# A linear-attention and feed-forward kernel: its steps put into an order written out for each engine, with whole query loads, one mask multiply and tables built on GpSimd

## The chip, the cores and the metric

The kernel runs on one core of a Trainium2 chip. A core has five engines that run side by side and meet through semaphores: TensorE (PE, matrix products; PEld is its loading of weights), VectorE (DVE), ScalarE (ACT), GpSimd (POOL) and SyncE (SP, which here only issues transfers). Sixteen DMA engines move data between HBM and the core's memory SBUF. Matrix products are written to PSUM, which has eight banks. The metric is the time of one execution on the device in microseconds (us); lower is better.

## The reference

Inputs are q, k, v of shape (4, 8, 768, 64) (batch, heads, positions, head size), a decay `lam` for each head, and the feed-forward weights `w_in` (512 x 2048), `w_out` (2048 x 512) and `alpha` (2048). All are float32.

```python
# attention, for each batch and head, in blocks of 64 positions
intra = (qb @ kb.T * Dmask) @ vb              # Dmask[i,j] = lam**(i-j) for i >= j, else 0
inter = (qb * lam_pow) @ kv_state             # lam_pow[i] = lam**(i+1)
out   = intra + inter
kv_state = lam**64 * kv_state + (kb * rev_pow).T @ vb
# feed-forward over the 3072 positions, x = heads side by side (512 columns)
h = x @ w_in
s = sin(alpha * h)
g = h + s * s / (alpha + 1e-9)
return g @ w_out
```

## The kernel before

**Units and groups.** The attention works in blocks of 128 positions in place of 64, two blocks (256 positions) at a time. One *unit* is one batch, four heads and 256 positions: 24 units, `u` = 0 to 23. Four units fill one *group* `g` of 512 rows for the feed-forward part: groups 0 to 5. `where(u)` gives the mapping. Rows of a unit are held with even and odd positions apart (`two`, `par`).

**Steps of a unit** (names as in the order of steps, with the unit's number behind them):

- `ld..q`, `ld..k`, `ld..v`: loads of 256 KB each on SP's queue into one of three buffers per kind (`load`). Before, the queries of units 1 to 7 (the set `Q4`) came as two transfers of 64 partitions each, in runs of 1024 B; all others come as one transfer in runs of 512 B.
- `cq`, `ck`: casts to bf16 (`cast`). `sv`: v times a table of inverse decays R, to bf16 (`scale_v`, on POOL).
- `tq`, `tk`: transposes on PE, and `e0`, `e1`: their copies out of PSUM, for units 0 to 8. For units 9 to 23 there is one DMA transpose instead, `dt`, on SP's queue (`turn_dma`).
- `sc`: scores, 16 small products into a pair of PSUM banks `s`. `m0`, `m1`: the causal mask, one multiply on DVE for each half of the scores (`domask`); the results are bf16.
- `kv`: the products of keys and scaled values. `bx` or `d0`, `d1`, `n0`, `n1`, `kc`: decay and carrying of the state, with copies on ACT and arithmetic on POOL (DVE for `bx` of units 3 to 7).
- `in`, `io`: products of the carried state and of the masked scores into the pair of banks `okv`. `oe`: the result times a table ET, into `xt` of the group (`outev`, DVE).
- From unit 8 on, `step` u is one PE block: the `in` and `io` products of unit u-1 and the `sc` and `kv` products of unit u.

**Steps of a group.** `f1_g_f`: one of 16 first products (four matmuls of 128x512 into one of four banks `f`; group 0's `f` = 0 comes in two halves, of units 0 and 1, and of units 2 and 3). `sn`: the sine on ACT. `sq`: the square, on ACT or POOL. `g`: the sum into `gall` on DVE, which frees the bank. `f2_g_m_j`: a quarter of one of the four second products of a group (again four matmuls of 128x512). `ev`: its copy on ACT into one of three buffers `ob`. `out`: its store, two transfers on SP's queue. The last one, `f2_5_3`, comes in two halves of 256 columns (`end0`, `end1`, `send0`, `send1`; `make_f2_end`, `f2send`); `send1` has one transfer on SP and one on ACT.

**Weights.** `wi0` to `wi3` (columns of `w_in`: 256, 512, 512, 768) and `wo0` to `wo3` (four of 16 row blocks of `w_out` each) are loaded by transfers that POOL issues and that cast to bf16.

**Tables.** `lamb` spreads `lam` over the partitions by a product on PE, `tabc` copies it out, `tab1` raises it to powers (POOL), `tabm` and `tab2` make E and its inverse R (DVE). `tabd` multiplies an identity that PE has put into PSUM (`eye`) with E on DVE, giving ED, and `tab0` spreads this over partitions by a product; `tab3` and `tab4` copy it out as ET and LBD.

**Matmuls without a reader.** 35 matmuls on constants (`warm`, tile `bz`): nine of 512 columns ahead of everything, 26 of 256 columns that a planner places.

**What sets the order.** All steps are created as `Op`s with the engines they may run on, what they wait for and which buffers they take and give back. `Plan.run` walks through time by its own costs and picks, for each engine that is free, the ready step with the lowest due time `vt`; `TUNE` shifts due times step by step and fixes engines. The steps are then emitted in that order, and each engine executes its instructions strictly in the order emitted, waiting on semaphores where needed. SP's queue is such an order too: what stands behind a waiting issue waits with it. `GATES` holds unit 5's first load until `wo1` has landed, and unit 8's until `f1_0_8` has run.

The chip sees no trace of the planner but the resulting order. In it PE has, around the first feed-forward tile:

```
... in1 io1 tq4 sc3 kv3 tk4 in2 io2 warm x5 in3 io3 f1_0_0_0 kv4 sc4 f1_0_0_1 in4 f1_0_1 ...
```

and the ends of SP's and ACT's orders are

```
SP:  ... out_5_2 out_5_0 send0 out_5_1 send1
ACT: ... ev_5_2 ev_5_0 end0 ev_5_1
```

Of the kernel before, what the change touches and what calls it, by code (L numbers as in the profile page):

```python
# [16 lines left out]
class Op:  # L17


    def __init__(self, name, cost, after, vt, emit, take=(), give=(), lag=0.08, mode=None,  # L20
                 dma=None, gives=None, behind=None, drain=9):
        self.name, self.cost, self.vt, self.emit = name, cost, vt, emit
        self.after = [a for a in after if a is not None]
        self.take, self.give, self.lag, self.mode = take, give, lag, mode
        self.dma, self.gives, self.owed, self.behind = dma, gives or {}, {}, behind
        self.drain = drain
        self.start = self.done = self.eng = self.lent = None
        self.bank, self.ins = {}, None


class Plan:
# [3 lines left out]
    BEGIN, LAND, DEPTH = {"SP": 0.4, "POOL": 2.0}, 1.7, 6  # L35
    HEAD = 0.75
    FETCH = (14.5, 20.5, 27, 48, 56, 66.5, 76.5, 86, 98.5, 108.5, 121, 131.5, 142.5, 157)
# [10 lines left out]
    def run(self):  # L48
        kids, left, ready_t = {}, {}, {}
        for op in self.ops:  # L50
            left[op] = len(set(op.after))
            ready_t[op] = 0.0
            for a in set(op.after):
                kids.setdefault(a, []).append(op)
        seq = {op: i for i, op in enumerate(self.ops)}
        pool = {e: [] for e in self.ENG}
        future = [(0.0, seq[op], op) for op in self.ops if not left[op]]
        heapq.heapify(future)
        free = dict.fromkeys(self.ENG, self.HEAD)
        queue = {"SP": [], "POOL": []}  # L60
        returns, order = [], []
        t, last, mode, n = 0.0, 0.0, None, 0

        def finish(op, at):
            op.done = at
            for who, kind in op.give:
                who.owed[kind] = who.owed.get(kind, who.gives.get(kind, 1)) - 1
                if not who.owed[kind]:
                    for b in who.bank[kind]:
                        heapq.heappush(returns, (at, kind, b))  # L70
            for k in kids.get(op, ()):
                ready_t[k] = max(ready_t[k], at + op.lag)
                left[k] -= 1
                if not left[k]:
                    heapq.heappush(future, (ready_t[k], seq[k], k))

        landing, flying = [], [0]

        def active(at):
            act = [q for q in queue.values() if q and q[0][1] <= at + 1e-9]  # L80
            return act, sum(q[0][0].dma[1] for q in act)

        while n < len(self.ops):
            while last < t - 1e-9:
                act, whole = active(last)
# [11 lines left out]
                for q in act:  # L97
                    q[0][2] -= rate * step * q[0][0].dma[1] / whole
                    if q[0][2] <= 1e-6:
                        op, land = q.pop(0)[0], last + step + self.LAND  # L100
                        finish(op, land)
                        if op.eng == "SP":
                            heapq.heappush(landing, land)
                            flying[0] -= 1
# [6 lines left out]
            while future and future[0][0] <= t + 1e-9:  # L111
                op = heapq.heappop(future)[2]
                for e, _ in op.cost:
                    heapq.heappush(pool[e], (op.vt, seq[op], op))
            for e in self.ENG:
                if free[e] > t + 1e-9:
                    continue
                kept, got = [], None
                while pool[e]:
                    item = heapq.heappop(pool[e])  # L120
                    op = item[2]
                    if op.start is not None:
                        continue
                    if all(len(self.banks[k]) >= op.take.count(k) for k in op.take) and (
                            op.behind is None or op.behind.start is not None) and (
                            e != "SP" or (flying[0] <= op.drain and
                                          flying[0] + len(landing) < self.DEPTH)):
                        got = op
                        break
                    kept.append(item)  # L130
                    if e == "SP" and flying[0] > op.drain:
                        break
                for item in kept:
                    heapq.heappush(pool[e], item)
                if got is None:
                    continue
                op, c = got, dict(got.cost)[e]
                if e == "PE" and op.mode is not None:
                    c += 0.09 * (op.mode != mode)
# [7 lines left out]
                n += 1  # L147
                if op.dma:
                    queue[e].append([op, t + c + self.BEGIN[e], op.dma[0]])
                    flying[0] += e == "SP"  # L150
                else:
                    finish(op, t + c)
            nxt = [v for v in free.values() if v > t + 1e-9]
            nxt += [x[0][0] for x in (future, returns) if x]
            act, whole = active(t)
            nxt += [t + q[0][2] * whole / q[0][0].dma[1] for q in act]
            nxt += [f + x for f in self.FETCH for x in (0, self.HOLD)]
            nxt += landing[:1]
            nxt += [q[0][1] for q in queue.values() if q and q[0][1] > t + 1e-9]
            nxt = [v for v in nxt if v > t + 1e-9]  # L160
            if not nxt:
                raise RuntimeError("stuck: " + ", ".join(o.name for o in self.ops if o.start is None)[:500])
            t = min(nxt)
# [4 lines left out]
def kernel(  # L168
# [26 lines left out]
    SF = set()  # L195
    TUNE = {
        "lam": (990.8, 'ACT'), "iden": (0.3, 'POOL'), "eye": (0, 'PE'), "lamb": (7.8, 'PE'),
        "tabc": (388.5, 'DVE'), "tab1": (40.4, 'POOL'), "tabm": (448, 'DVE'), "tabd": (-18.6, 'DVE'),
        "tab2": (-57.7, 'DVE'), "tab0": (-7.6, 'PE'), "tab4": (19.8, 'DVE'), "tab3": (6.2, 'ACT'),
        "alq": (957.4, 'ACT'), "alpha": (-8.9, 'PE'), "alphav": (-46.8, 'DVE'), "ld0q": (-7.4, 'SP'),  # L200
# [1150 lines left out]
```

## Time and profile before

| what | value |
|---|---|
| median of 3 runs | 219.5 us |
| all runs | 221.01, 219.5, 218.84 us |
| span of the profiled execution, first to last instruction | 218.1 us |
| the profiled execution's own time | not listed apart from the three runs; the span is 1.4 us below their median |
| PE busy | 205.9 us (94%), 2042 matmuls in the records |
| ACT / DVE / POOL busy | 140.4 / 124.6 / 122.8 us |
| moved by DMA | 33.65 MB in 60460 packets, mean 154 GB/s |

The profile is one execution. "Busy" is the time in which an engine runs an instruction; an engine at 94% over the whole span can still wait in one stretch and be the limit in another, so the prediction cuts the span into stretches. The clock row gives the TensorE clock that was granted, in tenths (9 is 90% or more). Some matmul records are missing from the trace, so counts of matmuls are a little low. A line such as "L717 POOL CAST qk<-st_k" names the source line, the engine, the operation, and what is written from what.

### The profile page before, as it was taken

What the parts mean: (1) busy time and instruction counts of PE and PEld (TensorE: products, weight loads), DVE (VectorE), ACT (ScalarE), POOL (GpSimd) and SP (SyncE); (2) the same over time, 40 slices, a digit from 0 to 9 for tenths busy, and PEclk for the clock granted to TensorE, in tenths of its full rate; (3) what the DMA queues carried; (4) which work ended last, traced back from release to release, by engine and by line L of the source; (5) the groups of instructions that cost most, each with busy time, mean ns of one, the idle gap of its engine ahead of it and who ended that gap; (6) DMA issues with size and microseconds to landing.
All of it is one profiled execution on the core that took longest, in us unless ns stands there. A gap on an engine that the chain in (4) does not pass through costs nothing.

```text
span 218.1 us, 5252 instructions
## 1 busy us (share of the span) xinstructions
PE 205.9 (94%) x2042; PEld 105.1 (48%) x2070; DVE 124.6 (57%) x203; ACT 140.4 (64%) x253; POOL 122.8 (56%) x201
## 2 busy tenths in 40 slices
PE   8786999999999999999999999999999999999992
PEld 3354544455536554455645545445445444444461
DVE  3678686537659973477767864738625643543000
ACT  4374698575499754876948778558726877775111
POOL 4569699948999999988899591313111001030000
PEclk9999999999999999999999999999999999999999
DMA  5999999998999992899999992202222022111253
GB/s 168 254 256 217 207 200 215 259 255 233 291 174 181 298 314 64 174 263 195 290 219 223 298 186 49 48 3 50 48 51 48 2 51 48 28 37 35 48 120 72
DMA packets 60460, 33.65 MB, mean 154 GB/s; under 512 B 18051, under 2 KB 57491, under 8 KB 60435
## 3 DMA queue, kind: packets, MB, share of 16 engines
q1 hardware_dynamic: 56096, 29.04, 59.1%
q0 software_dynamic: 4224, 4.19, 11.7%
q8 instruction: 16, 0.26, 0.5%
q10 hardware_dynamic: 114, 0.07, 0.1%
q14 instruction: 10, 0.07, 0.1%
HBM read 27.27 MB, written 6.29 MB: 154 GB/s over the span
## 4 chain that ended last, share of the span: by engine, by line
PE 70%; DMA 13%; POOL 6%; ACT 4%; issue 3%; SPq 2%; DVE 1%; POOLq 0%; ACTq 0%; DVEq 0%
PE ops L962 30%; PE hps L926 28%; DMA st_v<-in_v_dram 7%; DMA st_k<-in_k_dram 6%; PE okv L962 3%; PE sp L773 2%; PE okv L896 2%; SPq L698 2%; ACT s L933 2%; POOL qk L717 2%; PE okv L883 1%; POOL vb L723 1%; DVE gall L945 1%; ACT s L940 1%; POOL s L942 1%
## 5 line engine op out<-in xcount | busy, mean ns | idle before, releaser
L945 DVE SCALAR_TENSOR_TENSOR gall<-s,r_sb,hps 128x512 bf16<-128x512 bf16 (+1 forms) x97 | 70.1, 740 | 55.0 <-ACT s L940 33.9
L926 PE MATMUL hps<-xt,w_in_sb 128*128 128x512 bf16 (+1 forms) x371 | 90.6, 377 | 1.9 <-DVE gall L945 0.5
L933 ACT ACTIVATE s<-hps,alpha_sb 128x512 bf16<-128x512 f32 (+1 forms) x97 | 64.6, 679 | 34.4 <-PE hps L926 31.1
L962 PE MATMUL ops<-w_out_sb,gall 128*128 128x512 bf16 (+1 forms) x358 | 81.6, 370 | 1.0 <-issue 0.6
L962 PEld LDWEIGHTS <-gall 128*128 128x128 bf16 x400 | 38.3, 98 | 41.4
L926 PEld LDWEIGHTS <-w_in_sb 128*128 128x128 bf16 x388 | 36.7, 98 | 44.3 <-issue 2.7
L942 POOL TENSOR_TENSOR s<-s 128x512 bf16<-128x512 bf16 x24 | 24.8, 1041 | 39.7 <-ACT s L933 39.6
L940 ACT ACTIVATE s<-s 128x512 bf16<-128x512 bf16 (+1 forms) x73 | 44.5, 623 | 1.4
L782 DVE TENSOR_TENSOR sm<-sp,mask 128x512 bf16<-128x512 f32 x48 | 32.6, 684 | 6.1 <-PE sp L773 6.1
L723 POOL TENSOR_TENSOR vb<-st_v,R 128x512 bf16<-128x512 f32 x24 | 25.0, 1045 | 8.6 <-DMA st_v<-in_v_dram 6.2
L968 ACT COPY ob<-ops 128x512 f32<-128x512 f32 x21 | 12.2, 582 | 19.1 <-PE ops L962 18.9
L832 POOL TENSOR_TENSOR kvx<-kva,kvs 128x128 f32<-128x128 f32 x32 | 14.6, 457 | 14.8 <-ACT kva L817 14.5
L835 POOL TENSOR_TENSOR kvbd<-kvx,LBD 128x256 bf16<-128x256 f32 x32 | 19.6, 614 | 2.5
L913 DVE TENSOR_TENSOR xt<-okv,ET 128x512 bf16<-128x512 f32 x24 | 16.5, 686 | 3.5 <-PE okv L896 3.5
L999 PE MATMUL bz<-const-bfloat16-1.0 128*128 128x256 bf16 (+1 forms) x35 | 9.6, 343 | 1.7 <-PEq L1335 0.8
L717 POOL CAST qk<-st_q 128x512 bf16<-128x512 f32 x16 | 9.6, 614 | 1.4 <-PE okv L807 1.4
L773 PE MATMUL sp<-qt 64*64 64x128 bf16 x384 | 10.0, 221 | 0.0
L717 POOL CAST qk<-st_k 128x512 bf16<-128x512 f32 x16 | 9.7, 615 | 0.0
L896 PE MATMUL okv<-sm,vb 64*64 64x128 bf16 x384 | 9.7, 218 | 0.0
L873 POOL TENSOR_TENSOR kvs<-kvx,ET 128x128 f32<-128x128 f32 x24 | 9.5, 405 | 0.0
L883 PEld LDWEIGHTS <-kvbd 128*128 128x128 bf16 x80 | 6.2, 98 | 5.6 <-POOL kvbd L835 1.1
L883 PE MATMUL okv<-qt,kvbd 128*128 128x128 bf16 x80 | 8.6, 219 | 0.3 <-POOL kvbd L835 0.3
(64 smaller groups left out, 104.4 us busy)
## 6 DMA issues: line engine op xcount, KB each, us to landing
st_k<-in_k_dram SPq DMA_DIRECT2D x24, 256.0 KB, 5.2
st_v<-in_v_dram SPq DMA_DIRECT2D x24, 256.0 KB, 4.9
out_dram<-ob SPq DMA_DIRECT2D x46, 128.0 KB, 2.4
st_q<-in_q_dram SPq DMA_DIRECT2D x17, 256.0 KB, 5.2
w_out_sb<-in_moe_w_out_dram POOLq DMA_DIRECT2D x4, 512.0 KB, 14.4
st_q<-in_q_dram SPq DMA_DIRECT2D x14, 128.0 KB, 5.6
w_in_sb<-in_moe_w_in_dram POOLq DMA_DIRECT2D x2, 512.0 KB, 7.8
w_in_sb<-in_moe_w_in_dram POOLq DMA_DIRECT2D x1, 768.0 KB, 10.6
```

The costliest lines, as they stand in the source:

```text
L717: ENGINE[op.eng].tensor_copy(out=o, in_=i)
L723: ENGINE[op.eng].tensor_tensor(out=T[u, "vb"][:], in0=T[u, "v"][:].rearrange("p h two e -> p two h e"), in1=R[:, :, hs].unsqueeze(3).to_br ...
L782: V.tensor_tensor(out=T[u, "sm"][:, hd], in0=T[u, "sp"][hd][:], in1=mask[:].unsqueeze(2).to_broadcast([P, 2, 2, P]), op=ALU.mult)
L835: G.tensor_tensor(out=bd[:], in0=X.unsqueeze(2).to_broadcast([P, 2, 2, D]), in1=LBD[:, hs, :].unsqueeze(3).to_broadcast([P, 2, 2, D]), op= ...
L883: nc.tensor.matmul(out=okv[:, c, hp * P:(hp + 1) * P], lhsT=sts[c][:, hp].rearrange("p two e -> p (two e)"), rhs=T[u, "qt"][:, 0, :, hp, h ...
L913: V.tensor_tensor(out=xt[g][:, 2 * hh:2 * hh + 2, bb, :, :].rearrange("p hp c i -> p c hp i"), in0=T[u, "op"][:, :, 0:2 * P].rearrange("p ...
L926: op.ins = nc.tensor.matmul(out=op.tile[:, cols], lhsT=w_in_sb[:, c, f * P:(f + 1) * P], rhs=xt[g][:, c].rearrange("p b c i -> p (b c i)") ...
L933: A.activation(out=op.tile[:, cols], in_=mm.tile[:, cols], func=ACTF.Sin, scale=alpha_sb[:, f:f + 1])
L940: A.activation(out=op.tile[:, cols], in_=s1, func=ACTF.Square)
L942: ENGINE[op.eng].tensor_tensor(out=op.tile[:, cols], in0=s1, in1=s1, op=ALU.mult)
L945: V.scalar_tensor_tensor(out=gall[g][:, f, cols], in0=sq.tile[:, cols], scalar=r_sb[:, f:f + 1], in1=mm.tile[:, cols], op0=ALU.mult, op1=A ...
L962: op.ins = nc.tensor.matmul(out=first.tile[:, cols], lhsT=gall[g][:, f, m * P:(m + 1) * P], rhs=w_out_sb[:, f, cols], start=(f == 0), stop ...
```

## The change

- **Queries in one transfer.** The set `Q4` goes: the queries of all units are one transfer in 512 B runs. In `load` the buffer is written as one run of 2 KB on each partition. Casts, transposes and copies of those units lose their rearranged forms.
- **One mask multiply.** The scores of a unit are one tile over the pair of banks, the mask is stored twice as wide, and `mm` takes the place of `m0` and `m1`.
- **Tables on GpSimd.** The identity is made on POOL (`tabi`) in SBUF, not by PE in PSUM (`eye` goes); `tabd` with its three instructions runs on POOL.
- **Orders written out.** `vt`, `TUNE`, and the rules about which step follows which go. `SEQ` lists all steps for PE, DVE, ACT, POOL and SP; `Plan.run(SEQ)` only interleaves them and assigns buffers. Steps may have other engines than before: of the casts of units 1 to 7 seven move from ACT to POOL and `ck0` to DVE, and ten casts of later units move from POOL to ACT.
- **More buffers for the feed-forward part:** `gall` has four in place of three (`NGB`), so second products may come later; the second products of group 2 are split over the time up to the end. At most three second products (`part`) are open at once.
- **Matmuls without a reader:** 33, placed by `SEQ`, all ahead of `f1_0_0_0`; they share a tile where they follow each other in a bank.

The core of the diff:

```diff
-        if i == 0 and u in Q4:
-            for x in reversed(range(2)):
-                op.ins = SY.dma_start(
-                    out=tl[half[x]].rearrange("p h two e -> p (h two e)")
-                    .rearrange("p (g y) -> p g y", g=2),
-                    in_=src[2 * x:2 * x + 2].rearrange("g (p j) e -> p g (j e)", j=4))
...
-        else:
-            op.ins = SY.dma_start(
-                out=tl[:].rearrange("p h two e -> p h (two e)"),
-                in_=src.rearrange("h (p two) e -> p h (two e)", two=2))
+        op.ins = SY.dma_start(
+            out=tl[:].rearrange("p h two e -> p (h two e)"),
+            in_=src.rearrange("h (p two) e -> p h (two e)", two=2))
...
-    def domask(op, u, hd):
-        if hd == 0:
-            T[u, "sm"] = slot(op, work, "sm", [P, 2, 2, 2, P], BF16)
-        V.tensor_tensor(out=T[u, "sm"][:, hd], in0=T[u, "sp"][hd][:],
-                        in1=mask[:].unsqueeze(2).to_broadcast([P, 2, 2, P]), op=ALU.mult)
+    def domask(op, u):
+        T[u, "sm"] = slot(op, work, "sm", [P, 2, 2, 2, P], BF16)
+        V.tensor_tensor(out=T[u, "sm"][:].rearrange("p hd par hp i -> p (hd par) hp i"),
+                        in0=T[u, "sp"][:].rearrange("p hd par hp i -> p (hd par) hp i"),
+                        in1=mask[:].unsqueeze(2).to_broadcast([P, 4, 2, P]), op=ALU.mult)
...
+    def tables_i(op):
+        for c in range(2):
+            make_identity(nc, id2[half[c], :])
+
     def tables_d(op):
         for hd in range(2):
-            V.tensor_copy(out=E2[half[hd]], in_=E[half[hd]]
+            G.tensor_copy(out=E2[half[hd]], in_=E[half[hd]]
...
-        V.tensor_tensor(out=ED[:], in0=tbe.tile[:].unsqueeze(1).to_broadcast([P, HP * 2, D]),
+        G.tensor_tensor(out=ED[:], in0=id2[:].unsqueeze(1).to_broadcast([P, HP * 2, D]),
...
     def bank(op, kind, shape, dt, name, n=0):
-        return ps.tile(shape, dt, name=name, tag=op.bank[kind][n])
+        tag = op.bank[kind][n]
+        if name != "bz" or name not in latest.get(tag, {}):
+            latest[tag] = {name: ps.tile(shape, dt, name=name, tag=tag)}
+        return latest[tag][name]
...
-    for op in plan.run():
+    for op in plan.run(SEQ):
         op.emit(op)
```

The parts of `SEQ` that the prediction speaks of (`_None` left out of names):

```
PE, start:   warm x4 lamb warm x11 tq0 warm alpha tk0 warm x3 tq1 warm tab0 kv0 sc0 tk1 warm tq2
             warm x3 sc1 warm tk2 kv1 in0 io0 sc2 warm kv2 warm in1 tq3 io1 warm tk3 in2 io2 sc3
             kv3 warm x2 tq4 in3 warm x3 io3 f1_0_0_0 tk4 f1_0_0_1 f1_0_1 sc4 kv4 f1_0_5 in4 ...
PE, end:     ... f2_5_1_2 f2_5_0_0 f2_5_1_3 f2_5_3_0b f2_5_3_1b f2_5_0_1 f2_5_0_2 f2_5_0_3
             f2_5_3_2b f2_5_3_3b
DVE, start:  tabc tabm tab2 ck0 alphav tab4 mm0 e02 mm1 oe0 mm2 oe1 e13 oe2 bx3 mm3 oe3 e14 ...
ACT, start:  lam alq cq0 e00 cq1 e01 e10 kc0 tab3 e11 ck2 e12 kc1 cq3 kc2 ck3 e03 cq4 e04 kc3 ...
ACT, end:    ... ev_5_2 end0 ev_5_1 ev_5_0
POOL, start: iden tab1 tabi tabd sv0 ck1 cq2 bx0 sv1 wi0 sv2 bx1 wi1 bx2 sv3 wi2 wi3 ck4 n03 d13
             sv4 wo0 sq_0_1 sq_0_5 sq_0_2 wo1 sq_0_4 sq_0_8 wo2 n02 wo3 ...
SP, start:   ld0k ld0q ld1q ld0v ld1k ld2q ld1v ld2k ld2v ld3q ld3v ld3k ld4q ld4k ld4v | ld5q ld5k
             ld6q ld6k ld5v ld6v ld7q ld7k ld7v ld11v ld8q ld9q ld9k ld9v out_0_0 ld8v out_0_3
             ld10q ld8k ld10k ld10v ld11q dt9 ld12q ld11k ld12v ld16v ld16k dt10 ld16q ld13q ld12k
             ld13v dt11 ld15q ld13k dt12 ld14q out_0_2 ld15k ld15v ld14k dt13 ...
SP, end:     ... out_5_2 out_5_1 send1 send0 out_5_0
```

More of the change, by code (lines that the diff above doesn't have):

```diff
@@ L69, in finish @@
                     for b in who.bank[kind]:
-                        heapq.heappush(returns, (at, kind, b))
+                        heapq.heappush(returns, (when, kind, b))
             for k in kids.get(op, ()):
-                ready_t[k] = max(ready_t[k], at + op.lag)
+                ready[k] = max(ready[k], when + op.lag)
                 left[k] -= 1
[L74 to L83, printed above, removed]
+        while len(order) < len(self.ops):
             while last < t - 1e-9:
-                act, whole = active(last)
+                act = [q for q in queue.values() if q and q[0][1] <= last + 1e-9]
+                whole = sum(q[0][0].dma[1] for q in act)
                 step, rate = t - last, 1.0
@@ L618, in lam_all @@
         nc.tensor.matmul(out=op.tile[:], lhsT=row[:], rhs=lam_r[:], start=True, stop=True)
-    def eye(op):
-        op.tile = bank(op, "f", [P, D], FP32, "ey")
-        for c in range(2):
-            nc.tensor.matmul(out=op.tile[:], lhsT=iden[:], rhs=iden[:, half[c]],
-                             start=(c == 0), stop=(c == 1))
     def tables_c(op):
@@ L727, in turn_pe @@
     def turn_pe(op, u, j):
[L728 to L731 removed]
+        op.tile = bank(op, "f", [P, 2, 2, P], BF16, "pt")
         if j == 0:
             T[u, "qt"] = slot(op, work, "qt", [P, 2, 2, 2, P], BF16)
[L734 to L740 removed]
         for par in range(2):
@@ L1024 @@
+    for i in range(SEQ["PE"].split().count("warm") - NWARM):
+        dop = add("warm", on("PE", 0.11), [], dummy, take=("f",), mode="n")
         dop.give, dop.part = ((dop, "f"),), 2
     io_done = {}
-    sv_ops, cqs = {}, {}
     decs = {}
```

443 lines of the change are left out of this document (177 added, 266 removed), and 373 rows, old and new, of tables (SEQ, TUNE).

## The prediction

> **What bounds the kernel now.** The first view is the profile's page, the second the table of windows, cut at the first matmul of the feed-forward part (22.34 us) and at the end of the last matmul that has a reader (213.93 us). Its columns are length, busy time and count of PE, PEld, DVE, ACT and POOL, granted clock, DMA share, GB/s.
>
> ```profile
> span 218.1 us, 5252 instructions
> PE 205.9 (94%) x2042; PEld 105.1 (48%) x2070; DVE 124.6 (57%) x203; ACT 140.4 (64%) x253; POOL 122.8 (56%) x201
> PEclk9999999999999999999999999999999999999999
> 0.00:22.34 22.34, 17.31 (x282) 9.53 (x282) 13.84 (x37) 11.43 (x24) 14.75 (x28) 1.00 1.06 223
> 22.34:213.93 191.59, 188.49 (x1768) 95.57 (x1789) 110.34 (x165) 128.94 (x229) 108.05 (x174) 1.00 0.68 148
> 213.93:218.10 4.17, 0.11 (x2) 0.00 (x0) 0.42 (x1) 0.00 (x0) 0.00 (x0) 1.00 0.41 94
> 4.00:16.00 12.00, 9.42 (x170) 5.51 (x170) 7.88 (x21) 6.89 (x17) 6.79 (x7) 1.00 1.14 253
> 24.00:34.00 10.00, 9.61 (x56) 4.05 (x56) 7.01 (x12) 9.00 (x17) 7.73 (x15) 1.00 1.21 204
> ```
>
> Three stretches with three limits. From 22.34 to 213.93 PE is busy 188.5 of 191.6 us: its work alone sets the time, and only 3.1 us of idle can be won back. Ahead of it lie 22.3 us in which PE waits for data; behind it 4.2 us in which the last output is copied and stored. No other engine is near its limit on average, but the DMA engines are full for the first 35 us: 253 GB/s while q, k and v come in, 204 GB/s (counted at the written size) while the weights do.
>
> The chain of waits (start, length, what) shows what ends the first stretch, and the timelines show the work behind it:
>
> ```profile
> 11.76 7.27 DMA st_k<-in_k_dram
> 19.06 0.63 ACT qk L715
> 19.73 0.41 PE pt L743 x4
> 20.17 0.60 ACT qt L753
> ...
> 22.34 0.61 PE L926 MATMUL hps<-xt,w_in_sb 128*128 128x256 bf16 x4
> 22.88 0.32 PE L807 MATMUL kp<-vb,qk 64*64 64x64 bf16 x16
> 23.03 0.40 PE L773 MATMUL sp<-qt 64*64 64x128 bf16 x16
> 23.36 0.61 PE L926 MATMUL hps<-xt,w_in_sb 128*128 128x256 bf16 x4
> ```
>
> The key tile of 11.76 is unit 4's. Units 0 to 3 alone feed the first feed-forward group, but PE's order has unit 4's transposes (19.73) ahead of unit 2's output, so PE waits for a transfer that the group does not need.
>
> **The change, part by part.**
>
> *PE's work.* Both kernels have the same 96 first and 96 second products of four 128x512 matmuls, the same transposes, scores and steps. The 64-column identity matmuls (two) go, 35 matmuls without a reader become 33. So the 191.6 us stretch stays, apart from its idle time and from where it starts and what follows.
>
> *Start: who waits for what.* In the new order in2, io2, sc3 and kv3 come ahead of unit 4's tq4, and tk4 stands behind the first feed-forward tile, so unit 3's data set the start. Its key transfer is the twelfth in SP's order; the tenth and thirteenth (queries of 3 and 4) can be read from the casts that waited for them:
>
> ```profile
> 13.88 0.62 ACT L715 CAST qk<-st_q 128x512 bf16<-128x512 f32 x1 [0.88 <-DMA st_q<-in_q_dram]
> 17.10 0.62 ACT L715 CAST qk<-st_q 128x512 bf16<-128x512 f32 x1 [0.44 <-DMA st_q<-in_q_dram]
> 19.17 0.41 DVE L849 TENSOR_TENSOR kvbd<-kp,LBD 128x256 bf16<-128x256 f32 x1
> 20.64 0.69 DVE L913 TENSOR_TENSOR xt<-okv,ET 128x512 bf16<-128x512 f32 x1 [0.46 <-PE okv L896]
> L782 DVE TENSOR_TENSOR sm<-sp,mask 128x512 bf16<-128x512 f32 x48 | 32.6, 684 | 6.1 <-PE sp L773 6.1
> ```
>
> That is (17.10-13.88)/3 = 1.07 us a transfer, and 13.88+2x1.07 = 16.0 for the twelfth. From there: cast 0.62, transposes and handovers 0.5, then DVE one thing after another: copy e13 0.42, wait for io2 0.2, xt of unit 2 0.69, kvbd 0.41, the mask, then PE's io3 with handovers 0.57, and xt of unit 3 0.69. The one mask multiply of 128x1024 has no row; above stands twice 0.684 = 1.37, below the growth between 128x256 (0.41) and 128x512 (0.684) carried on, 0.684+2x0.27 = 1.23. I take 1.3. The sum is 5.4, so f1_0_0_1 runs at 21.4. Before it ran at 23.36, with unit 4's kv4 and sc4 done just ahead (0.5, the rows at 22.88 and 23.03), which the new order still owes: **gain 23.36-0.5-21.4 = 1.4 us**. Bounds: if only DVE's chain from the tenth transfer counted, 3.0; if the handovers each cost 0.1 more and the weights slow the twelfth transfer by 0.5, 0.4.
>
> *Tables on GpSimd.* These lie beside that chain as long as POOL is in time with unit 3's values.
>
> ```profile
> 1.85 0.39 POOL masks.py:199 TENSOR_SCALAR_AFFINE_SELECT iden<-iden 128x128 bf16<-128x128 bf16 x1
> 4.92 1.67 POOL L630 TENSOR_TENSOR E<-lam_bc,pos 128x8 f32<-128x8 f32 x1 [2.36 <-DVE lam_bc L627]
> 8.87 2.07 POOL L723 TENSOR_TENSOR vb<-st_v,R 128x512 bf16<-128x512 f32 x2 [2.28 <-DVE R L637]
> 12.96 1.04 POOL L723 TENSOR_TENSOR vb<-st_v,R 128x512 bf16<-128x512 f32 x1 [2.01 <-DMA st_v<-in_v_dram]
> 14.51 1.72 POOL L672 DMA_DIRECT2D w_in_sb<-in_moe_w_in_dram  x2
> L717 POOL CAST qk<-st_k 128x512 bf16<-128x512 f32 x16 | 9.7, 615 | 0.0
> ```
>
> The power table can start up to 0.9 earlier, since lamb stands behind four of the nine wide matmuls: it ends at 5.7 to 6.6. The identity (two of about 0.39) and ED with its two small copies (one of the 1.04 kind, 0.4) add 2.2, so sv0 ends at 9.0 to 9.9 (before 9.9). Two casts (0.62 each), bx0 (0.6) and sv1 (1.04) bring the first weight load to 11.8 to 12.7, before 14.51. sv2 still waits for its data until 12.96; bx1, wi1, bx2, sv3 follow and end near 17.1, while kv3 is wanted at about 18. Hidden, with 0.9 to spare; gone, it would cost what it is late.
>
> *Queries in 512 B pieces.* One issue in place of two on SP, some 0.7 us for each of seven; the transfers, not the issues, set the pace (253 GB/s is 1.04 us for 256 KB), so nothing is gained. The price of smaller pieces is bounded by zero and by the difference between 1.07 and 1.04 for each transfer, below 0.1 for unit 3's: no term.
>
> *The stream behind it.* The new order wants steps 9 to 18 earlier, and each needs a DMA transpose that stands in SP's queue behind other loads:
>
> ```profile
> 35.24 1.26 SPq L690 DMA_DIRECT2D st_q<-in_q_dram  x2
> 70.59 1.80 SPq L759 DMA_TRANSPOSE qt<-qk  x1
> qt<-qk SPq DMA_TRANSPOSE x15, 4.4
> 79.68 0.39 PE L883 MATMUL okv<-qt,kvbd 128*128 128x128 bf16 x4
> ```
>
> Loading goes on at 35.24, when the second quarter of w_out has landed; that gate stays, and the weights' stream has no slack to land sooner. The transpose issued at 70.59 (unit 12's) stands behind 28 loads, one output and three transposes counted from there; PE used it at 79.68. In the new order unit 11's stands behind 29 loads, two outputs and two transposes, so it is issued at about 71 and lands 4.4 later, 75.4. PE has 52 products (0.863 each, 44.9) and 9.5 us of attention between its first feed-forward tile, now near 20.7, and step 11: it wants the tile at 75.1. Units 13 and 14 come out as close. What was 5 us of slack is gone. I take a stall of 0.3; bounds 0 and, if every transfer ran 5% slower than in this comparison over some 80 us, 4.
>
> *Idle time on PE.* The 3.1 us are many small waits. A new order may lose those on other engines:
>
> ```profile
> PE hps L926 <- DVE gall L945: 0.5, 2, 0.3
> PE hps L926 <- ACT kva L861: 0.2, 1, 0.2
> ```
>
> Bounds 0 and 0.7; I take 0.3 as gain, about the middle.
>
> *Tail.* The last part of the new SP order is out_5_1, send1, send0, out_5_0; before it was send0, out_5_1, send1. send1 waits for the last copy, so two issues of send0 and two of out_5_0, both ready earlier, now queue behind it:
>
> ```profile
> 210.07 1.10 SPq L983 DMA_DIRECT2D out_dram<-ob  x2
> 213.31 1.11 SPq L990 DMA_DIRECT2D out_dram<-ob  x2
> 214.03 0.42 DVE L976 COPY ob<-ops 128x256 f32<-128x256 f32 x1 [14.63 <-PE ops L962]
> 214.51 0.55 SPq L983 DMA_DIRECT2D out_dram<-ob  x1
> ```
>
> The last issue starts 0.55+1.10+0.55 = **2.2 us later** after the last matmul, and nothing covers it. I see no bound far from this: 2.0 to 2.4.
>
> *Matmuls without a reader.* Those that are left stand where PE waits for unit 0 to 3. Their cost is covered by that wait. The row of the clock shows 9 throughout; the first nine such matmuls, though, start 0.42 us apart, where a feed-forward matmul takes 0.216.
>
> ```profile
> 1.15 0.15 PEld L999 LDWEIGHTS <-const-bfloat16-1.0 128*128 128x128 bf16 x1 [0.27 <-issue]
> 1.57 0.15 PEld L999 LDWEIGHTS <-const-bfloat16-1.0 128*128 128x128 bf16 x1 [0.28 <-issue]
> ```
>
> So there is a slow state early on. The Trainium skill, "TensorE: Matmul & The Clock Gate", section "Why this matters for your kernels", says that a gap of more than about 3 us without matmuls brings the clock back to half. By that rule a longer early gap would cost, as an estimate from the page's 3.4 us window, 1.7 us; the trace has no such gap after 4 us, so it does not show it. From rows: PE's longest early wait in the new order is for tab0 and kv0, below 2 us, and at half rate the chain's matmuls (about 2 us) would cost 2 more.
>
> **Sum**, against the profiled span: 218.1 - 1.4 (start) - 0.3 (idle) + 0.3 (stream) + 2.2 (tail) = 218.9. The median of the runs shown, 219.5, lies 1.4 above the span; with the same around it, **220.3 us**, 0.4% above before. About 1% is what a measurement of this kernel can tell from no change: 217.3 to 221.7 counts as the same.
>
> **The rivals.**
>
> *The transposes come late* (slower). The start gains its 1.4, but steps 10 to 14 wait for unit 10 to 14's transposes, and PE, whose order is fixed, cannot do other products meanwhile. For it: the margin of about zero above, and that SP's order puts loads of units 16, 19 and 21 ahead of nearer ones. Against it: the stretch has PE idle for under 2% now although the DMA engines are as full. With 3.5 us instead of 0.3: 223.5. It decides from 1.5 us of stall on.
>
> *The start gains more* (not slower). Unit 3's chain starts from the tenth transfer and gives 3.0, the idle time 0.7, the stream keeps up, the tail costs 2.2: 218.1-3.0-0.7+2.2 = 216.6, so 218.0. For it: weights are issued 2 us sooner. Against it: keys of unit 3 are a transfer nobody can skip. Under 217.3 it comes only if the 512 B loads also run faster into their now flat destination; no row shows that form, and at the weights' reading rate (twice 204 GB/s) unit 3 would land 4 us sooner, and POOL's 17.1 would then hold the start: 217.0 with it.
>
> *The clock falls back early*: 2 more at the start, 222.3. Nothing in the trace speaks for it.
>
> **How the numbers follow.** Forecast 0.50, transposes late 0.25, start gains more 0.20 (most of it near 218, a good third at 217), clock 0.05. The forecast's own range is 218.3 to 222 from its bounds; the cases on both sides widen it to 217.0 to 223.5. Faster by over 1%: 0.17, mostly the flat load and what I have not seen; within 1%: 0.54; slower: 0.29, the first rival and part of the clock's and of the forecast's upper end.
>
> **What would show it.** In the new profile: the first feed-forward matmul near 20.7 and not 22.3, and the one at 21.4 behind it; the chain there through st_k of unit 3; the mask at 1.23 to 1.37 us; wi0 issued near 12. From the last matmul to the end 6.4 us and not 4.2, with five issues on SP behind the last copy. Waits of PE on DMA transposes under 1 us in sum. The prediction is wrong if the stretch between has over 193 us, if the first tile comes before 19.5 or after 22, or if the tail stays near 4.2.

## The result, and the profile after

The changed kernel takes 218.88 us (median of 20 executions, 218.33 to 220.60) against 219.64 for the kernel before (median of 20, 218.84 to 221.89): a ratio of 0.9956 with a 95% interval of 0.9935 to 0.9978. It is 0.4% faster. Forecast were 220.3 us and 0.4% slower; the time lies inside the range, on the other side of no change. Both profiled executions are single ones, and where a run lists both, the time is 1.7 to 1.8 above the span: the profiled execution of the changed kernel took 218.37 with a span of 216.6, half a microsecond below its median. So the two spans lie 1.5 apart, the two medians only 0.8. Every ratio here leaves out executions more than 1.5% above the fastest of their kernel; the only such one is the 223.04 us of the kernel with pairs below.

The page of the changed kernel:

```profile
span 216.6 us, 5232 instructions
PE 206.4 (95%) x2066; PEld 105.6 (49%) x2066; DVE 119.4 (55%) x174; ACT 139.1 (64%) x251; POOL 131.4 (61%) x212
PEclk9999999999999999999999999999999999999996
```

Its table of windows, cut like the one of before at the first feed-forward matmul (19.05) and at the end of the last matmul (209.73); columns as in the prediction:

```profile
0.00:19.05 19.05, 16.32 (x275) 9.66 (x275) 10.66 (x26) 10.69 (x24) 17.08 (x36) 1.00 1.07 245
19.05:209.73 190.68, 190.03 (x1798) 95.92 (x1792) 108.32 (x147) 128.44 (x227) 114.30 (x177) 1.00 0.69 149
209.73:216.60 6.87, 0.01 (x1) 0.00 (x0) 0.42 (x1) 0.00 (x0) 0.00 (x0) 0.72 0.35 79
4.00:16.00 12.00, 10.55 (x192) 6.53 (x190) 6.98 (x14) 8.27 (x19) 11.59 (x19) 1.00 1.20 290
```

The three stretches were 22.34, 191.59 and 4.17 us; they are 19.05, 190.68 and 6.87. The start gives 3.3, the stretch in which PE is full 0.9, and the tail takes 2.7 back: 1.5 in sum. The last row tells where to look: from 4 to 16 us the core moved 290 GB/s where it had moved 253. In the same stretch POOL is busy for 11.59 of the 12 us, where it had been for 6.79.

The timeline of the changed kernel up to the second feed-forward tile (start, length, engine, what):

```profile
14.39 0.62 ACT L490 CAST qk<-st_k 128x512 bf16<-128x512 f32 x1
15.07 0.39 PE L508 MATMUL pt<-iden,qk 128*128 128x128 bf16 x4
15.45 1.04 POOL L498 TENSOR_TENSOR vb<-st_v,R 128x512 bf16<-128x512 f32 x1
15.68 0.41 DVE L517 COPY qt<-pt 128x512 bf16<-128x512 bf16 x1
16.49 0.69 DVE L674 TENSOR_TENSOR xt<-okv,ET 128x512 bf16<-128x512 f32 x1 [0.39 <-PE okv L655]
16.59 0.34 PE L566 MATMUL kp<-vb,qk 64*64 64x64 bf16 x16
17.43 1.22 DVE L540 TENSOR_TENSOR sm<-sp,mask 128x1024 bf16<-128x1024 f32 x1
18.70 0.42 PE L655 MATMUL okv<-sm,vb 64*64 64x128 bf16 x16 [0.51 <-DVE sm L540]
19.05 0.61 PE L689 MATMUL hps<-xt,w_in_sb 128*128 128x256 bf16 x4
19.16 0.69 DVE L674 TENSOR_TENSOR xt<-okv,ET 128x512 bf16<-128x512 f32 x1 [0.52 <-PE okv L655]
19.72 0.82 PE L689 MATMUL hps<-xt,w_in_sb 128*128 128x256 bf16 x5
```

The cast at 14.39 is that of unit 3's keys, the twelfth transfer; it shows no wait for it. The second tile runs at 19.72, 5.33 later. The prediction had 16.0 for the transfer and 5.4 for the chain behind it: the transfer was there 1.6 sooner, and the time behind it came out. But the chain of waits that ends at the first tile is another one in this profile. Going back in time it leads from DVE's mask of unit 3 to the `xt` of unit 1 (15.07) and from there to POOL, which runs one instruction after another from 7.83 on (start, length, what):

```profile
10.56 1.00 POOL vb L498
11.56 0.90 POOL w_in_sb L456
12.49 1.07 POOL vb L498
15.07 0.70 DVE xt L674
```

These are `sv1`, the issue of `wi0`, `sv2` and the `xt`. From 7.83 on no transfer stands in this chain.

The tail of the changed kernel:

```profile
208.94 0.59 ACT L731 COPY ob<-ops 128x512 f32<-128x512 f32 x1 [2.92 <-PE ops L725]
209.83 0.42 DVE L739 COPY ob<-ops 128x256 f32<-128x256 f32 x1 [11.26 <-PE ops L725]
210.28 1.75 SPq L746 DMA_DIRECT2D out_dram<-ob  x3
210.28 0.55 ACTq L746 DMA_DIRECT2D out_dram<-ob  x1
212.47 1.11 SPq L753 DMA_DIRECT2D out_dram<-ob  x2
```

Five issues on SP stand behind the last copy (`send1`, two of `send0`, two of `out_5_0`). The last one ends at 213.58, and 3.0 later the span ends; before, the last issue ended at 215.06 and the span 3.0 later.

### The profile page after: what moved, and what is told of

It reads as the page before. It is cut to its first block, busy times and chain, and to the rows that moved or that the text cites. A ratio compares the mean times of both kernels' runs of the same rounds, so it can differ in the third digit from the quotient of the medians.

```text
span 216.6 us, 5232 instructions
## 1 busy us (share of the span) xinstructions
PE 206.4 (95%) x2066; PEld 105.6 (49%) x2066; DVE 119.4 (55%) x174; ACT 139.1 (64%) x251; POOL 131.4 (61%) x212
## 4 chain that ended last, share of the span: by engine, by line
PE 87%; POOL 5%; DVE 2%; issue 2%; ACT 1%; POOLq 0%; DVEq 0%
PE hps L689 38%; PE ops L725 35%; PE okv L725 3%; PE sp L532 3%; PE okv L655 3%; PE okv L642 2%; POOL vb L498 1%; DVE gall L708 1%; PE okv L566 1%; PE pt L508 1%; POOL E L410 1%; ACT s L696 1%; ACT s L703 1%; DVE sm L540 1%; POOL w_in_sb L456 0%
## 5 line engine op out<-in xcount | busy, mean ns | idle before, releaser
L689 PE MATMUL hps<-xt,w_in_sb 128*128 128x512 bf16 (+1 forms) x388 | 91.7, 377 | 0.7 <-DVE gall L708 0.6
L696 ACT ACTIVATE s<-hps,alpha_sb 128x512 bf16<-128x512 f32 (+1 forms) x97 | 65.5, 680 | 29.0 <-PE hps L689 27.5
L725 PE MATMUL ops<-w_out_sb,gall 128*128 128x512 bf16 (+1 forms) x368 | 83.1, 370 | 0.0
L705 POOL TENSOR_TENSOR s<-s 128x512 bf16<-128x512 bf16 x31 | 32.1, 1041 | 49.3 <-ACT s L696 47.2
L703 ACT ACTIVATE s<-s 128x512 bf16<-128x512 bf16 (+1 forms) x66 | 40.3, 621 | 1.2
L540 DVE TENSOR_TENSOR sm<-sp,mask 128x1024 bf16<-128x1024 f32 x24 | 29.2, 1218 | 1.0 <-PE sp L532 1.0
L492 POOL CAST qk<-st_k 128x512 bf16<-128x512 f32 x18 | 10.9, 614 | 3.3 <-DMA st_k<-in_k_dram 3.2
L490 ACT CAST qk<-st_q 128x512 bf16<-128x512 f32 x13 | 7.9, 619 | 3.1 <-DMA st_q<-in_q_dram 3.1
L576 ACT COPY kva<-okv 128x256 f32<-128x256 f32 (+1 forms) x16 | 5.1, 316 | 6.9 <-PE okv L566 6.9
L762 PE MATMUL bz<-const-bfloat16-1.0 128*128 128x256 bf16 (+1 forms) x33 | 8.3, 358 | 0.8 <-PEq L1056 0.8
```

Of the source, the lines that this page charges most:

```text
L540: V.tensor_tensor(out=T[u, "sm"][:].rearrange("p hd par hp i -> p (hd par) hp i"), in0=T[u, "sp"][:].rearrange("p hd par hp i -> p (hd par ...
L689: op.ins = nc.tensor.matmul(out=op.tile[:, cols], lhsT=w_in_sb[:, c, f * P:(f + 1) * P], rhs=xt[g][:, c].rearrange("p b c i -> p (b c i)") ...
L696: A.activation(out=op.tile[:, cols], in_=mm.tile[:, cols], func=ACTF.Sin, scale=alpha_sb[:, f:f + 1])
L703: A.activation(out=op.tile[:, cols], in_=s1, func=ACTF.Square)
L705: ENGINE[op.eng].tensor_tensor(out=op.tile[:, cols], in0=s1, in1=s1, op=ALU.mult)
L725: op.ins = nc.tensor.matmul(out=first.tile[:, cols], lhsT=gall[g][:, f, m * P:(m + 1) * P], rhs=w_out_sb[:, f, cols], start=(f == 0), stop ...
```

## The experiments

Two theories stood for the earlier transfers. One: loading the queries of units 1 to 7 in one transfer, not in two of 64 partitions, makes the transfers themselves faster. The other: the new orders keep SP's queue fuller, and the form of the loads does not matter. Each ratio compares a kernel with the kernel before, run beside it on the same chip. Differences between the medians of two changed kernels go in part across chips and are less sure.

**SP's tail in another order.**

```diff
-            "out_3_3 out_2_0 out_2_3 out_4_3 out_5_2 out_5_1 send1 send0 out_5_0 ",
+            "out_3_3 out_2_0 out_2_3 out_4_3 out_5_2 send0 out_5_1 out_5_0 send1 ",
```

> The changed kernel with the end of SP's order as out_5_2, send0, out_5_1, out_5_0, send1. Theory (the store issues queued behind the last copy set the end): last issue on SP starts at 210.7 instead of 213.0 and ends at 211.2; 3.0 us from there to the end of the span as in both kernels, so the span falls from 216.6 to 214.3 and the time from 218.9 to 216.5, 0.986 of before. Rival (the end is set by how long the stored data take, or by what lies around the span): under 0.7 us gained, time above 218.2.

Measured: 216.55 us, ratio 0.9845 (0.9806 to 0.9885). The tail of this kernel:

```profile
209.61 0.58 ACT L731 COPY ob<-ops 128x512 f32<-128x512 f32 x1 [2.92 <-PE ops L725]
210.50 0.42 DVE L739 COPY ob<-ops 128x256 f32<-128x256 f32 x1 [11.27 <-PE ops L725]
210.95 0.55 ACTq L746 DMA_DIRECT2D out_dram<-ob  x1
211.44 0.53 SPq L746 DMA_DIRECT2D out_dram<-ob  x1
```

One issue is left behind the last copy, and it ends at 211.97, 3.0 before the span of 215.0 does. The whole order of stores at the end is worth 218.88 - 216.55 = 2.3 us. The last issue still waits from 210.92, when its copy is done, to 211.44, because `out_5_0` is just ahead of it.

**Queries as before, in pairs of transfers.** The forms of `load`, `cast`, `turn_pe` and `turn_ev` for the set `Q4` come back into the changed kernel:

```diff
+    Q4 = set(range(1, 8))
...
+        if i == 0 and u in Q4:
+            for x in reversed(range(2)):
+                op.ins = SY.dma_start(
+                    out=tl[half[x]].rearrange("p h two e -> p (h two e)")
+                    .rearrange("p (g y) -> p g y", g=2),
+                    in_=src[2 * x:2 * x + 2].rearrange("g (p j) e -> p g (j e)", j=4))
```

> The changed kernel with the queries of units 1 to 7 loaded as before, in two transfers of 64 partitions with 1024 B runs each; all orders as in the changed kernel. Theory (whole query loads are what made the transfers 0.91 us apart and not 1.07): unit 3's keys land 1.0 to 1.6 us later than 14.4, the first feed-forward tile is at 20.0 to 20.6 instead of 19.05, time 219.8 to 220.5. Rival (the new order of issues and casts keeps the queue full and the form of the queries does not matter): first tile within 0.3 of 19.05, time 218.6 to 219.2.

Measured: 220.87 us (219.09 to 223.04), ratio 1.0026 (0.9991 to 1.0060). That is 2.0 above the changed kernel by the medians and 0.7%, or 1.5 us, by the ratios (1.0026 against 0.9956). In the profiled execution (221.73 us, one of the slower ones) the cast of unit 3's keys waits for their transfer until 16.36, and the first tile is at 21.23, both later than expected:

```profile
16.36 0.62 ACT L505 CAST qk<-st_k 128x512 bf16<-128x512 f32 x1 [1.22 <-DMA st_k<-in_k_dram]
21.23 0.66 PE L714 MATMUL hps<-xt,w_in_sb 128*128 128x256 bf16 x4
```

The first 20 us in slices of 0.5 us, GB/s by DMA, first the changed kernel, then this one:

```profile
GB/s 0 0 0 28 151 323 321 279 283 257 318 337 333 298 293 291 292 290 287 292 289 293 290 291 290 288 292 311 284 293 244 219 215 214 201 207 215 199 227 195
```

```profile
GB/s 0 0 0 36 153 321 338 311 157 245 227 179 278 295 298 170 216 183 169 285 292 292 292 264 164 221 178 203 290 297 264 161 211 187 228 207 214 224 259 265
```

The changed kernel holds about 290 (284 to 333) from the thirteenth slice to the thirtieth (6 to 15 us). With pairs the rate falls to 164 to 221 for a few slices at a time in the same stretch and comes back to 290 between. At about 200 GB/s 256 KB take 1.3 us, at 290 they take 0.9. The Trainium skill has this, in "SBUF — State Buffer", section "Door 1: The DMA port swizzle (why `[64,N]` ≈ `[32,N]`)": partitions 0 to 63 reach 8 of the 16 ports, as do 64 to 127, and it gives 196 GB/s for 64 partitions at 1 MiB against 328 for 128. The trace agrees in the size of the drop (164 to 221 against 290); it does not show the ports.

A small part is not transfers but clock: in the clock row of this page the fourth slice is lower, which it is not in the changed kernel; from 18 to 20 us the granted clock was 0.50, after 2 us (16 to 18) in which PE was busy for 0.92. From the cast of the keys to the second tile (21.95) it takes 5.59 here against 5.33, so 0.3 of the 2.2 us by which that tile is later can be the clock; 2.0 are the keys' transfer.

```profile
PEclk9996999999999999999999999999999999999996
```

**The target's form alone.** The flat target that the prediction's rival named goes back to four pieces:

```diff
-            out=tl[:].rearrange("p h two e -> p (h two e)"),
+            out=tl[:].rearrange("p h two e -> p h (two e)"),
```

> The changed kernel with the target of every q, k and v load written as four pieces of 512 B on a partition, as before, in place of one run of 2 KB. Theory (number of transfers decides): no change, transfers 0.90 apart, first tile at 19.05 within 0.2, time 218.6 to 219.2. Rival (the flat target makes the loads faster): transfers 1.0 apart or more, first tile at 20 or later, time from 219.8.

Measured: 218.95 us, ratio 0.9966 (0.9939 to 0.9994), first tile at 19.05. No effect: the flat target is not what makes the loads faster.

**The kernel before with whole queries.** Its own order of steps, step for step; only the form of seven loads changes, with their casts and copies.

```diff
-    Q4 = set(range(1, 8))
+    Q4 = set()
```

> The kernel before, in exactly its own order of steps, with the queries of units 1 to 7 loaded whole, as all others are. Theory (a load of 64 partitions runs at about 200 GB/s where one of 128 runs at 290): the keys of unit 4, behind which the first feed-forward tile stands there, land 1.2 to 1.6 us earlier than 19.04, the first tile is at 20.8 to 21.2 instead of 22.34, and the time is 217.8 to 218.5, below the changed kernel's 218.9, since its tail is the short one. Rival (the pairs cost only in the changed order): time 219.2 to 219.9.

Measured: 217.74 us, ratio 0.9894 (0.9854 to 0.9935): faster than the changed kernel. In its timeline the keys of unit 4, for which the cast waits, and the first tile:

```profile
17.03 0.62 ACT L716 CAST qk<-st_k 128x512 bf16<-128x512 f32 x1 [0.69 <-DMA st_k<-in_k_dram]
20.33 0.61 PE L927 MATMUL hps<-xt,w_in_sb 128*128 128x256 bf16 x4
```

Its windows, cut at the first tile and the last product:

```profile
20.33:211.66 191.33, 190.32 (x1796) 95.47 (x1789) 110.01 (x165) 128.72 (x229) 109.03 (x175) 1.00 0.67 150
211.66:215.80 4.14, 0.12 (x2) 0.00 (x0) 0.42 (x1) 0.00 (x0) 0.00 (x0) 1.00 0.42 95
```

The cast stood at 19.06 before and the first tile at 22.34: both come 2.0 earlier, more than the 1.2 to 1.6 expected, and the rest is that of before. So whole queries alone, without any other part of the change, make the kernel before 1.1% faster.

**What of the pairs is slow.** Two kernels load the same queries in two transfers with 512 B runs, one in halves of the partitions, one in halves of the heads.

```diff
+        for x in [half[1], half[0]]:
+            op.ins = SY.dma_start(
+                out=tl[x].rearrange("p h two e -> p (h two e)"),
+                in_=src.rearrange("h (p two) e -> p h (two e)", two=2)[x])
```

```diff
+        for x in [slice(2, 4), slice(0, 2)]:
+            op.ins = SY.dma_start(
+                out=tl[:, x].rearrange("p h two e -> p (h two e)"),
+                in_=src[x].rearrange("h (p two) e -> p h (two e)", two=2))
```

> The changed kernel with the queries of units 1 to 7 in two transfers of 64 partitions each, but in its own layout, in runs of 512 B. Theory (a transfer to 64 partitions runs slower, whatever its runs): as with the pairs of 1024 B, about 220 to 240 GB/s from 4 to 16 us in place of 290, first tile 1 to 2.2 later than 19.05 to 19.7, time 219.9 to 220.9. Rival (the runs of 1024 B are what is slow): 280 GB/s or more, first tile at 19.05 to 19.9, time 218.6 to 219.3.

> The changed kernel with the queries of units 1 to 7 in two transfers of 128 partitions and two heads each, in runs of 512 B. Theory (64 partitions are what is slow, not the count of transfers): 280 to 290 GB/s from 4 to 16 us, time 218.6 to 219.3. Rival (each further transfer costs 0.3 to 0.4): 250 GB/s or less, time from 219.9.

Measured: 222.41 us in halves of partitions (220.31 to 223.38), ratio 1.0143 (1.0090 to 1.0196); 218.75 us in halves of heads, ratio 0.9950 (0.9919 to 0.9981). The same row of GB/s, first for the partitions, then for the heads:

```profile
GB/s 0 0 0 37 97 317 335 327 152 222 256 230 290 275 279 217 224 220 239 292 291 291 287 219 207 217 233 290 289 294 184 211 234 225 204 233 300 270 223 204
```

```profile
GB/s 0 0 0 35 94 328 342 321 245 245 289 271 309 339 332 306 288 271 296 297 299 291 277 296 296 291 316 282 284 235 217 220 221 253 224 208 209 209 207 223
```

From 6 us to 14.5 us half the partitions bring the drops (207 to 239) and half the heads bring none (271 or more). The first tile is at 20.32 with half the partitions and at 19.03 with half the heads. Neither the number of transfers nor the 1024 B runs is the cause, the 64 partitions are. That the halves with 512 B runs are slower than the pairs with 1024 B, by 1.5 us in the medians, was not expected, and it stays open: there are four executions, and the profiled one, the fastest of them, does not show it.

**ED back on VectorE.**

```diff
-            "iden tab1 tabi tabd sv0 ck1 ...
+            "iden tab1 tabi sv0 ck1 ...
-            "tabc tabm tab2 ck0 alphav ...
+            "tabc tabm tab2 ck0 tabd alphav ...
```

> The changed kernel with ED's three instructions back on DVE (behind the identity, which stays on GpSimd). They take 1.0 there in place of 1.5 and sv0 can start at 7.1, when its values have landed, not at 7.83. Theory A (the keys of unit 3 at 14.4 and 5.35 us behind them set the first tile, POOL only runs alongside): first tile within 0.2 of 19.05, time 218.6 to 219.2. Theory B (GpSimd's row of tables, scaled values and weight issues sets the first tile): first tile 0.4 to 0.7 earlier, time 218.2 to 218.5.

Measured: 219.01 us, ratio 0.9962 (0.9933 to 0.9990), no effect; the first tile of this execution is at 19.69. The row of `sv0` on POOL:

```profile
7.79 1.04 POOL L498 TENSOR_TENSOR vb<-st_v,R 128x512 bf16<-128x512 f32 x1 [1.50 <-DMA st_v<-in_v_dram]
```

POOL now waits 1.5 us for the values, which landed later here than the 7.1 that was expected, and starts them where it started them behind the tables (7.83). In time the tables on GpSimd cost nothing that can be told from noise. But this profile does not refute the theory that POOL's row sets the first tile, since the loads were late in it: what the tables would cost with loads as early as in the changed kernel's profile is not shown.

**Two mask multiplies.**

```diff
-        V.tensor_tensor(out=T[u, "sm"][:].rearrange("p hd par hp i -> p (hd par) hp i"),
...
+        for hd in range(2):
+            V.tensor_tensor(out=T[u, "sm"][:, hd], in0=T[u, "sp"][:, hd],
+                            in1=mask[:, :2].unsqueeze(2).to_broadcast([P, 2, 2, P]),
+                            op=ALU.mult)
```

> The changed kernel with two mask multiplies of 128x512 for each unit in place of one of 128x1024, at the same place in DVE's order. Theory (DVE has room behind the start, and only unit 3's is on the chain to the first tile): two take 1.37 less overlap, 0.1 to 0.15 more than 1.22, time 218.8 to 219.2. Rival (the single multiply is worth more, since DVE's queue holds back PE's steps later on): waits of PE for DVE of over 0.7 us in sum behind the first tile, time above 219.5.

Measured: 218.98 us, ratio 0.9950 (0.9929 to 0.9970). The groups, first of the changed kernel, then of this one:

```profile
L540 DVE TENSOR_TENSOR sm<-sp,mask 128x1024 bf16<-128x1024 f32 x24 | 29.2, 1218 | 1.0 <-PE sp L532 1.0
```

```profile
L541 DVE TENSOR_TENSOR sm<-sp,mask 128x512 bf16<-128x512 f32 x48 | 30.7, 682 | 1.2 <-PE sp L532 1.2
```

1.5 us of DVE's time are saved over 24 units, and none of it shows in the end.

**Without the matmuls that fill the waits.** The 18 between the transposes of unit 0 and the first tile are left out.

```diff
-            "warm alpha tk0 warm warm warm tq1 warm tab0 kv0 sc0 tk1 warm tq2 warm warm warm sc1 "
+            "alpha tk0 tq1 tab0 kv0 sc0 tk1 tq2 sc1 "
...
```

> The changed kernel without the 18 matmuls without a reader that stand between the transposes of unit 0 and the first feed-forward tile; the 15 ahead of tq0 stay. Theory (they lie in stretches in which PE waits anyway, and the waits are too short for the clock to fall): first tile within 0.3 of 19.05 to 19.6, time 218.6 to 219.2. Rival (they keep the clock up): single matmuls of 128 columns before the first tile take twice as long, first tile 1 to 2 us later, time 219.9 to 221.

Measured: 219.53 us (218.42 to 221.36), ratio 0.9982 (0.9952 to 1.0013). The clock row of its page:

```profile
PEclk9985799999999999999999999999999999999996
```

Its windows (the clock is the third number from the right):

```profile
4.00:12.00 8.00, 5.37 (x81) 3.05 (x79) 3.51 (x10) 4.79 (x10) 7.31 (x14) 1.00 1.10 287
12.00:20.00 8.00, 6.24 (x153) 4.57 (x154) 5.75 (x8) 4.63 (x13) 6.96 (x10) 0.64 1.10 213
```

Its timeline, with its longest wait and its first tile:

```profile
7.72 0.40 PE L508 MATMUL pt<-iden,qk 128*128 128x128 bf16 x4 [1.38 <-ACT qk L490]
20.57 1.04 PE L689 MATMUL hps<-xt,w_in_sb 128*128 128x256 bf16 x4
```

In this execution, the slowest of twelve, the clock falls to a mean of 0.64 after a stretch in which PE is busy for 5.4 of 8 us, and the four matmuls of the first tile take 1.04 in place of 0.61. Its time is 221.36; executions whose mean clock is 0.995 or more take 218.42 to 219.41, those at 0.974 or less 220.03 to 221.36. So the rival's mechanism is real, in some executions and not in others; in the median it is 0.6 above the changed kernel, with intervals that overlap. The longest wait of PE before the fall is 1.4 us. The rule that the prediction cited from the Trainium skill ("TensorE: Matmul & The Clock Gate", "Why this matters for your kernels") names gaps of more than about 3 us as what brings the clock down; here it fell without one.

**Tail on both sides.** SP's new tail, and on PE:

```diff
-            "... f2_5_0_0 f2_5_1_3 f2_5_3_0b f2_5_3_1b f2_5_0_1 f2_5_0_2 f2_5_0_3 f2_5_3_2b f2_5_3_3b"
+            "... f2_5_0_0 f2_5_1_3 f2_5_0_1 f2_5_0_2 f2_5_0_3 f2_5_3_0b f2_5_3_1b f2_5_3_2b f2_5_3_3b"
```

> The kernel of the run with SP's new tail, and on PE the last three quarters of f2_5_0 ahead of f2_5_3_0b and f2_5_3_1b, so that f2_5_0 is done 0.86 earlier and its two issues are over when the last copy is. Theory (one issue after the last copy is all that is left): in the run with SP's new tail the last issue waited from 210.92 to 211.44, so 0.5 less, 216.05. Rival (the copy on ACT and its store then stand beside nothing that waits for them): 216.5.

Measured: 216.07 us (215.55 to 216.67), ratio 0.9819 (0.9780 to 0.9857), the fastest version here.

```profile
209.16 1.11 SPq L753 DMA_DIRECT2D out_dram<-ob  x2
210.31 0.42 DVE L739 COPY ob<-ops 128x256 f32<-128x256 f32 x1 [11.27 <-PE ops L725]
210.76 0.47 SPq L746 DMA_DIRECT2D out_dram<-ob  x1
```

The last issue now follows its copy at once. It beats both kernels: 2.8 us below the changed one, 1.8% below before.

## Why the prediction was wrong, point by point

- **Queries in 512 B pieces: the step that failed.** The prediction priced it at "below 0.1", "no term". It set the 1.07 us between two landings against the 1.04 that follow from 253 GB/s. But both numbers come from a queue in which every third load was a pair, so both hold the slow halves, and their difference could not show them. The price is 1.5 to 2.0 us in the new order (ratio 1.0026 against 0.9956; 220.87 against 218.88, with a small part for the clock), and no less in the old one (ratio 0.9894, which is 2.3 us; first tile 2.0 earlier). The row of slices was there to be read in the trace of before:

```profile
GB/s 0 0 0 43 118 333 334 285 185 263 295 241 221 213 284 305 288 205 249 224 281 291 291 212 245 230 267 291 296 231 238 227 282 278 236 198 209 213 207 212
```

 From 6 to 15 us it swings between 205 and 305. A mean of 253 hides a rate of 290 with holes in it.
- **Everything else, in sum, was about right.** With the pairs put back, the changed kernel has the ratio 1.0026 (0.9991 to 1.0060); the forecast was 220.3 over 219.5, 1.004. In its profile the keys end the wait at 16.36 (forecast 16.0) and the second tile runs at 21.95 (forecast 21.4): the path of the forecast is the path of that kernel. That the rest sums up so well is in part luck: in the profile of the changed kernel the tail was priced 0.5 too low and the stretch in which PE is full 0.9 too high.
- **Start.** Forecast: gain 1.4 at the second tile, first tile at 20.7. In the profile: the second tile at 19.72, a gain of 23.36 - 0.5 - 19.72 = 3.1, the first at 19.05, sooner than the 19.5 that was given as the bound. Of the 1.7 that are missing, 1.6 are the twelfth transfer. That the chain goes through unit 3's keys, one of the signs named, did not hold: with whole queries they land so early that the chain of waits goes through POOL instead (`sv1`, `wi0`, `sv2`). That the 5.33 us from the cast to the tile agree with the 5.4 is in part luck: up to unit 2's `xt` (16.49) it takes 2.1 where the sum had 1.7, behind it 3.2 where the sum had 3.7. What held is the order of work on DVE from that `xt` on. The kernel with whole queries in the old order has its first tile at 20.33, so the order alone brings it some 0.6 to 1.3 forward (19.05 to 19.69 in the profiles of the new order).
- **Mask.** Forecast 1.3, bounds 1.23 and 1.37; measured 1.218, just below the lower one, which carried on DVE's growth from 256 to 512 columns.
- **Tables on GpSimd.** No cost in time, as forecast, but not because POOL had time to spare: its row is part of the chain. The spare 0.9 was nearly used up, since the loads came sooner: unit 3's values were ready at 16.49, and their products ran at 16.59.
- **The stream behind.** Forecast 0.3 of stall; there was none. PE's waits behind the first tile, from the table of waits from 18 us on, hold no transfer:

```profile
PE hps L689 <- DVE gall L708: 0.6, 2, 0.3
PE okv L655 <- DVE sm L540: 0.5, 1, 0.5
```

 Step 11's transpose on SP and its first product, from the timeline:

```profile
68.43 1.37 SPq L521 DMA_TRANSPOSE qt<-qk  x1
74.70 0.39 PE L642 MATMUL okv<-qt,kvbd 128*128 128x128 bf16 x4
```

 Step 11 ran at 74.70, forecast 75.1; its transpose was issued at 68.43 and not at 71, since the loads ahead of it were faster. The rival of late transposes fell for the same reason. It is not far off: in the profiled execution with the old target form one transpose was 0.9 late.
- **Idle time on PE.** Forecast 0.3, bound 0.7; the stretch is 0.9 shorter. In other profiles it is 190.8 (SP's new tail) against 191.3 (whole queries in the old order), 0.5 apart. Which small waits went is not settled: both traces list nearly the same ones.
- **Tail.** Forecast 2.2 (2.0 to 2.4), in the profile 6.87 - 4.17 = 2.7, and 2.3 in time when SP's order is mended. The five issues are there; the sum left out 0.44 between the end of `send0`'s second issue (212.03) and the next (212.47); it is 0.1 in the profiles of the kernels with split query loads, and why is open.
- **Forecast against the span.** The time outside it is 1.75, not 1.4; by that the profiled execution of before took about 219.9, a little more than its median. The forecast's own range of 218.3 to 222 is not the sum of its bounds: all the low ones together give 217.8 and all the high ones 225.5.
- **The rivals.** "The start gains more" came true in its size (3.1 for its 3.0), but not for its reason: it let the chain start from the tenth transfer, and the chain passes no transfer of unit 3. Faster loads it tied to the flat target, which the run with the old target shows to be wrong. What it said of POOL, that its row would then hold the start, is what the chain shows. "The clock falls back early" had 0.05 and did not happen here; one run shows that it does where the filling matmuls are gone.

## What to carry to other kernels

A mean rate over a stretch in which two kinds of transfers alternate prices neither of them: take the row of slices, find the highest rate that is held, and ask what runs in the holes. A load that fills all 128 partitions is worth more than longer runs on 64. At the end of a kernel, the store that becomes ready last belongs last in its queue, and nothing that was ready earlier behind it.

## What the runs showed of the hardware that was not expected

- While loads to 64 partitions were in the queue the rate fell to 164 to 239 GB/s, where loads to 128 alone held 290, with runs of 512 B and of 1024 B alike; two transfers of 128 partitions and half the bytes cost nothing against one (218.75 against 218.88).
- In a tail without matmuls the granted clock falls when the tail is long: 0.72 over 6.87 us, 1.00 over 4.17 and 4.14.
- With PE busy for about two thirds of 8 us and no wait above 1.4 us the clock fell, to a mean of 0.64 over the next 8 us, in one execution, and the mean over the whole execution was 0.995 or more in others of the same kernel.
